# A 32-byte pad under the right side of SBUF in a rope attention and two-FFN kernel

## The chip, the core and the metric

The kernel runs on one core of one Trainium2 chip. The metric is the device time of one execution in microseconds, as a median over executions. The reference is computed in fp32; the kernel gets there by splitting fp32 operands into a high and a low part in the fp32r type and adding three products.

## What is computed

```python
# q, k, v: (4, 8, 576, 64)
q_rot, k_rot = rotate(q), rotate(k)                     # rope
attn = softmax(q_rot @ k_rot^T / 8)
x = (attn @ v) as (2304 tokens, 512)
h = x @ w_in      ; x = (h - tanh(h)) @ w_out           # w_in 512x2048, w_out 2048x512
h = x @ w_in2     ; out = (h * sigmoid(h)) @ w_out2
```

## The kernel before

**Attention** takes the 32 heads as 16 pairs. A pair has nine score tiles; each is built from 288-column matmuls of `qs` (stationary) with `kh` and `kl` (moving), lines 364, 365 and 371, and is followed by row maximum, exponential, transposes and the product with v. Even and odd pairs keep their rotated q and k in different pools: `qk_even` on the right side of SBUF, `qk_odd` on the left side. The rope work that builds them (pool `rope`) is on the right side too.

**The FFNs** are four passes p: passes 0 and 1 are the two halves of the first FFN's hidden dimension, passes 2 and 3 those of the second. A pass takes five token blocks kb in the order of the table `ORDER` (four of 512 tokens and block 4 with 256), and for each block eight slices f of 128 hidden units. One (p, kb, f) is a tick m, 160 in all. Tick m issues, on TensorE,

- `gemm_h(m)`, line 685: 12 matmuls hp <- x, w_in. Moving: `xh`, `xl` (512 columns, 256 in block 4). Stationary: `win`.
- `gemm_out(m - 4)`, line 761: in passes 0 and 1 12 matmuls with `gh`, `gl` moving and `wout` stationary; in passes 2 and 3 the roles are exchanged: `wout` moving, always 512 columns, and `gh`, `gl` stationary (12 matmuls, 6 in block 4).

Between them ScalarE and VectorE turn hp into g and its high and low parts (lines 696 to 730), and convert the next weights (lines 121 to 153). The order on each engine is written out by hand. An hp tile has four buffers, and `gemm_out` runs four ticks behind.

Where operands lie decides the case. The x of a block is split into `xh`, `xl` by `split` (lines 664 to 674), and line 666 alternates the pool from block to block:

```python
fp = pools["sb" if x % 2 == 0 else "x"]
```

`pools["sb"]` is `ffn`, on the right side; `pools["x"]` is `ffn_x`, on the left. The x of one block is kept where the next pass begins with the same block. So the pools go, in the order of the work:

| pass | blocks in order | pool of xh, xl |
|---|---|---|
| 0 | 0, 1, 4, 2, 3 | ffn, ffn_x, ffn, ffn_x, ffn |
| 1 | 3, 0, 1, 4, 2 | ffn, ffn_x, ffn, ffn_x, ffn |
| 2 | 0, 1, 4, 2, 3 | ffn_x, ffn, ffn_x, ffn, ffn_x |
| 3 | 3, 0, 1, 2, 4 | ffn_x, ffn, ffn_x, ffn, ffn_x |

`gh` and `gl` are always in `ffn`. The weights are in `wearly` and `wlate`, on the left. The first byte in a partition, as the pools give it out:

| tile (pool, side) | first byte before | modulo 64 |
|---|---|---|
| win, first slot (wearly, left) | 35520 | 0 |
| win, late slot (wlate, left) | 101056 | 0 |
| xh0 (ffn_x, left) | 158400 | 0 |
| xin (ffn, right) | 176096 | 32 |
| xh0 (ffn, right) | 184288 | 32 |
| gh (ffn, right) | 217056 | 32 |
| qs, kh (qk_odd, left) | 156544, 161152 | 0, 0 |
| qs, kh (qk_even, right) | 215008, 219616 | 32, 32 |

All tiles of a pool start at the same place modulo 64, and all steps inside them that a matmul takes (512 bytes in a weight or a g, 1152 and 2304 in q and k) are multiples of 64.

Of the kernel before, what the change touches and what calls it, by code (L numbers as in the profile page):

```python
# [8 lines left out]
F32 = mybir.dt.float32  # L9
# [20 lines left out]
def kernel(  # L30
# [43 lines left out]
    make_identity(nc, ident)  # L74
    sqa = const.tile([128, 1], F32, name="sqa")
    ht2 = const.tile([128, 1], F32, name="ht2")
    dram = ctx.enter_context(tc.tile_pool(name="dram", bufs=1, space=bass.MemoryType.DRAM))

    xd = [[dram.tile([128, KD, TW[kb]], F32, name=f"xd{l}{kb}") for kb in range(NBLK)] for l in range(2)]
# [820 lines left out]
```

## Time and profile before

| what | us |
|---|---|
| median of 3 runs (1147.18 to 1148.46) | 1147.21 |
| span of the profiled execution, first to last instruction | 1145.9 |
| TensorE busy in it | 1119.5 |
| VectorE busy | 785.3 |
| ScalarE busy | 659.2 |
| GpSimd busy | 268.4 |

The median of the timed runs is 1.3 us above the span of the profiled execution. TensorE's busy time is no measure of its use: matmuls overlap, a 512-column one is shown with some 394 ns while the next begins much sooner. The pace is read from the starts of successive matmuls in the timeline, which lists instructions in order of time and merges equal neighbours (x2). There a tick is the time from one first `hp<-xh` to the next.

### The profile page before, as it was taken

What the parts mean: (1) busy time and instruction counts of PE and PEld (TensorE: products, weight loads), DVE (VectorE), ACT (ScalarE), POOL (GpSimd) and SP (SyncE); (2) the same over time, 40 slices, a digit from 0 to 9 for tenths busy, and PEclk for the clock granted to TensorE, in tenths of its full rate; (3) what the DMA queues carried; (4) which work ended last, traced back from release to release, by engine and by line L of the source; (5) the groups of instructions that cost most, each with busy time, mean ns of one, the idle gap of its engine ahead of it and who ended that gap; (6) DMA issues with size and microseconds to landing.
All of it is one profiled execution on the core that took longest, in us unless ns stands there. A gap on an engine that the chain in (4) does not pass through costs nothing.

```text
span 1145.9 us, 16928 instructions
## 1 busy us (share of the span) xinstructions
PE 1119.5 (98%) x6032; PEld 902.6 (79%) x6032; DVE 785.3 (69%) x1385; ACT 659.2 (58%) x1431; POOL 268.4 (23%) x359
## 2 busy tenths in 40 slices
PE   5999999999999999999999999999999999999998
PEld 4777777777778889888888898888888888888887
DVE  7778788787858978888899979876544533323323
ACT  4888888788866757766666657534343323222221
POOL 6566676666300101111001001111000000000000
PEclk9999999999999999999999999999999999999999
DMA  4133323232311223221333332432232203122012
GB/s 130 47 99 84 113 68 110 89 94 86 100 64 42 92 74 111 96 89 56 111 129 110 111 120 84 147 111 92 75 110 74 74 1 111 37 74 93 31 44 74
DMA packets 69588, 98.94 MB, mean 86 GB/s; under 512 B 13952, under 2 KB 50432, under 8 KB 67712
## 3 DMA queue, kind: packets, MB, share of 16 engines
q1 hardware_dynamic: 69344, 97.61, 26.3%
q8 instruction: 47, 0.77, 0.3%
q14 instruction: 37, 0.30, 0.1%
q10 hardware_dynamic: 160, 0.26, 0.1%
HBM read 74.25 MB, written 23.59 MB: 85 GB/s over the span
## 4 chain that ended last, share of the span: by engine, by line
PE 91%; DVE 4%; ACT 3%; issue 1%; DMA 0%; SPq 0%; POOL 0%; DVEq 0%; ACTq 0%
PE acc L761 35%; PE hp L685 35%; PE x L498 7%; PE tpp L466 4%; PE sc L364 3%; PE sc L365 2%; PE tpq L332 2%; PE sc L371 1%; ACT p L391 1%; DVE st L377 1%; ACT kh L346 1%; PE sc L446 1%; PE tpb L418 0%; DMA xm<-in_q_dram 0%; DVE wa L136 0%
## 5 line engine op out<-in xcount | busy, mean ns | idle before, releaser
L685 PE MATMUL hp<-xh,win 128*128 128x512 f32 (+1 forms) x1280 | 391.7, 371 | 0.0
L696 ACT ACTIVATE t<-hp 128x512 f32<-128x512 f32 (+1 forms) x160 | 89.0, 557 | 409.7 <-PE hp L685 400.0
L730 DVE TENSOR_TENSOR gl<-t,gh 128x512 fp32r<-128x512 f32 (+1 forms) x160 | 105.9, 662 | 259.5 <-ACT gh L728 259.2
L685 PEld LDWEIGHTS hp<-xh,win 128*128 128x128 f32 x1280 | 233.7, 188 | 46.8 <-issue 1.3
L685 PE MATMUL hp<-xl,win 128*128 128x512 f32 (+1 forms) x640 | 237.0, 370 | 0.0
L761 PE MATMUL acc<-gh,wout 128*128 128x512 f32 (+1 forms) x640 | 196.7, 372 | 1.2 <-ACT u L700 1.2
L761 PE MATMUL acc<-wout,gh 128*128 128x512 f32 x576 | 181.0, 395 | 0.0
L377 DVE TENSOR_REDUCE st<-sc 128x1 f32<-128x576 f32 x144 | 108.7, 755 | 60.0 <-PE sc L446 34.9
L685 PEld LDWEIGHTS hp<-xl,win 128*128 128x128 f32 x640 | 120.2, 188 | 23.2
L761 PEld LDWEIGHTS acc<-gh,wout 128*128 128x128 f32 x640 | 116.7, 188 | 24.9 <-ACT u L700 1.6
L761 PEld LDWEIGHTS acc<-wout,gh 128*128 128x128 f32 x576 | 107.1, 188 | 24.4
L761 PE MATMUL acc<-gl,wout 128*128 128x512 f32 (+1 forms) x320 | 118.9, 372 | 0.0
L153 POOL TENSOR_TENSOR win<-wa,win 128x512 fp32r<-128x512 f32 x32 | 45.4, 1419 | 292.5 <-ACT win L149 292.5
L761 PE MATMUL acc<-wout,gl 128*128 128x512 f32 x288 | 113.8, 395 | 0.0
L391 ACT ACTIVATE p<-sc,st 128x576 f32<-128x576 f32 x144 | 107.0, 743 | 9.4 <-DVE pr L434 7.2
L153 POOL TENSOR_TENSOR wout<-wa,wout 128x512 fp32r<-128x512 f32 x32 | 43.8, 1367 | 284.2 <-ACT wout L149 272.5
L432 ACT ACTIVATE pt<-tpp 128x512 f32<-128x512 f32 x144 | 86.1, 598 | 28.2 <-PE tpp L466 27.4
L728 ACT ACTIVATE gh<-t 128x512 fp32r<-128x512 f32 (+1 forms) x160 | 93.7, 586 | 1.5 <-PE acc L761 1.5
L364 PE MATMUL sc<-kh,qs 128*128 128x288 f32 x256 | 85.4, 348 | 7.1 <-ACT p L391 5.1
L466 PE MATMUL tpp<-ident,p 128*128 128x128 f32 x576 | 87.1, 274 | 0.0
L498 PE MATMUL x<-pt,vm 128*64 128x256 f32 (+1 forms) x512 | 75.8, 418 | 2.1 <-DVE xs L507 1.9
L364 PEld LDWEIGHTS sc<-kh,qs 128*128 128x128 f32 x256 | 49.2, 192 | 34.2 <-ACT p L391 17.8
(112 smaller groups left out, 1798.5 us busy)
## 6 DMA issues: line engine op xcount, KB each, us to landing
raw<-in_moe_w_in_dram SPq DMA_DIRECT2D x32, 512.0 KB, 3.6
raw<-in_moe_w_out_dram SPq DMA_DIRECT2D x32, 512.0 KB, 3.6
xin<-xd SPq DMA_DIRECT2D x14, 1024.0 KB, 4.8
pd<-xo SPq DMA_DIRECT2D x34, 256.0 KB, 2.7
xo<-pd SPq DMA_DIRECT2D x34, 256.0 KB, 4.9
xm<-in_k_dram SPq DMA_DIRECT2D x16, 256.0 KB, 2.9
xm<-in_q_dram SPq DMA_DIRECT2D x16, 256.0 KB, 3.0
vm<-in_v_dram SPq DMA_DIRECT2D x16, 256.0 KB, 2.9
```

The source lines that it names most:

```text
L153: POOL.tensor_tensor(out=w[:, 1], in0=self.val.pop(j), in1=w[:, 0].bitcast(F32), op=ALU.subtract)
L364: PE.matmul(sc[:, e, 0:HALF], lhsT=l, rhs=kh[:, c], start=True, stop=False)
L377: DVE.tensor_reduce(out=st, in_=s_t[g][:, :, 0:HALF], op=ALU.max, axis=AX.XY, negate=True)
L391: ACT.activation(out=p.rearrange("p (e s) -> p e s", e=2), in_=sc[:, :, 0:HALF], func=ACTF.Exp, bias=st, accum_out=sum_t[i][:, n:n + 1])
L432: ACT.activation(out=dst, in_=src, func=ACTF.Copy)
L466: PE.transpose(tp[:, cc * 128:(cc + 1) * 128], p[:, p0 + cc * 128:p0 + (cc + 1) * 128], ident)
L498: PE.matmul(x[o, 0:w], lhsT=l, rhs=r, start=(cc == 0), stop=(cc == NJ))
L685: PE.matmul(hp, lhsT=w[:, a, ws], rhs=bb, start=(n == 0), stop=(n == 3 * KD - 1))
L696: ACT.activation(out=t, in_=hp, func=ACTF.Tanh, scale=0.5 if l else 1.0)
L728: ACT.activation(out=gh, in_=t, func=ACTF.Copy)
L730: DVE.tensor_tensor(out=gl, in0=t, in1=gh.bitcast(F32), op=ALU.subtract)
L761: PE.matmul(acc, lhsT=a, rhs=bb, start=(fi == 0 and n == 0), stop=(fi == NH - 1 and n == 2))
```

## The change

A pool with one tile of 8 fp32 elements (32 bytes in each partition) is opened on the right side of SBUF before all other pools of that side. The right side grows downwards, so every tile on it (pools `qk_even`, `rope`, `ffn`) starts 32 bytes lower: xh0 at 184256, gh at 217024, kh of the even pairs at 219584, all multiples of 64. The left side does not move. No instruction reads or writes the pad; every engine has the same instructions in the same order with the same waits as before.

```diff
@@ -74,6 +74,8 @@
     make_identity(nc, ident)
     sqa = const.tile([128, 1], F32, name="sqa")
     ht2 = const.tile([128, 1], F32, name="ht2")
+    right_pad = ctx.enter_context(tc.tile_pool(name="right_pad", bufs=1, side="right"))
+    right_pad.tile([128, 8], F32, name="pad_right")
     dram = ctx.enter_context(tc.tile_pool(name="dram", bufs=1, space=bass.MemoryType.DRAM))
```

## Rows read from the trace of the kernel before

**Rows 1.** The page: span, lines of the chain that ended last, granted TensorE clock.

```profile
span 1145.9 us, 16928 instructions
...
PE acc L761 35%; PE hp L685 35%; PE x L498 7%; PE tpp L466 4%; PE sc L364 3%; PE sc L365 2%; PE tpq L332 2%; PE sc L371 1%; ACT p L391 1%; DVE st L377 1%; ACT kh L346 1%; PE sc L446 1%; PE tpb L418 0%; DMA xm<-in_q_dram 0%; DVE wa L136 0%
```

**Rows 2.** TensorE's waits from 345 us on: releaser, total us, times, longest.

```profile
PE acc L761 <- ACT u L700: 1.2, 1, 1.2
```

**Rows 3.** Timeline of TensorE in pass 3, block 0 (x in ffn): start, us, instruction.

```profile
979.09 0.39 PE L685 MATMUL hp<-xh,win 128*128 128x512 f32 x1
979.32 0.40 PE L685 MATMUL hp<-xl,win 128*128 128x512 f32 x1
...
981.66 0.39 PE L685 MATMUL hp<-xh,win 128*128 128x512 f32 x1
981.89 0.63 PE L761 MATMUL acc<-wout,gh 128*128 128x512 f32 x2
...
984.69 0.39 PE L685 MATMUL hp<-xh,win 128*128 128x512 f32 x1
```

**Rows 4.** Timeline of TensorE in pass 2, block 3 (x in ffn_x).

```profile
896.12 0.39 PE L685 MATMUL hp<-xh,win 128*128 128x512 f32 x1
896.35 0.39 PE L685 MATMUL hp<-xl,win 128*128 128x512 f32 x1
...
898.62 0.40 PE L685 MATMUL hp<-xh,win 128*128 128x512 f32 x1
...
901.65 0.39 PE L685 MATMUL hp<-xh,win 128*128 128x512 f32 x1
```

**Rows 5.** Timeline of TensorE in pass 1, block 2 (x in ffn): one gemm_out.

```profile
714.58 0.40 PE L761 MATMUL acc<-gh,wout 128*128 128x512 f32 x1
...
717.38 0.40 PE L685 MATMUL hp<-xh,win 128*128 128x512 f32 x1
```

**Rows 6.** Timeline of TensorE in pass 0, block 1 (x in ffn_x): one tick.

```profile
374.76 0.40 PE L685 MATMUL hp<-xh,win 128*128 128x512 f32 x1
...
380.32 0.40 PE L685 MATMUL hp<-xh,win 128*128 128x512 f32 x1
```

**Rows 7.** Timeline of TensorE, 256 columns: pass 0 block 4 (ffn), pass 3 block 4 (ffn_x).

```profile
430.51 0.28 PE L685 MATMUL hp<-xh,win 128*128 128x256 f32 x1
...
433.34 0.28 PE L685 MATMUL hp<-xh,win 128*128 128x256 f32 x1
...
1108.26 0.40 PE L685 MATMUL hp<-xh,win 128*128 128x256 f32 x2
...
1108.74 0.63 PE L761 MATMUL acc<-wout,gh 128*128 128x512 f32 x2
```

**Rows 8.** Timeline of TensorE in attention: first scores of pairs 8 to 12.

```profile
169.38 0.40 PE L364 MATMUL sc<-kh,qs 128*128 128x288 f32 x1
...
189.04 0.40 PE L364 MATMUL sc<-kh,qs 128*128 128x288 f32 x1
...
208.99 0.38 PE L364 MATMUL sc<-kh,qs 128*128 128x288 f32 x1
...
229.14 0.38 PE L364 MATMUL sc<-kh,qs 128*128 128x288 f32 x1
...
248.56 0.38 PE L364 MATMUL sc<-kh,qs 128*128 128x288 f32 x1
```

**Rows 9.** Waits of the other engines from 345 us on.

```profile
ACT t L696 <- PE hp L685: 394.6, 150, 4.5
...
DVE gl L730 <- ACT gh L728: 256.5, 111, 4.3
```

**Rows 10.** Busy us by engine from 540 to 640 us: PE, PEld, DVE, ACT, POOL, then clock.

```profile
540.00:640.00 100.00, 100.00 (x432) 80.61 (x431) 91.06 (x143) 66.97 (x122) 12.33 (x9) 1.00 0.33 107
```

## Prediction

> **What bounds the kernel now.** I read the chain first, then TensorE's waits, then the spacing of its matmuls. In the chain that ended last two FFN lines alone hold 70% of the span, 761 and 685, both on TensorE [rows 1]. From 345 us to the end TensorE waits once, for 1.2 us [rows 2]; the other engines wait for it instead: ScalarE 394.6 us in 150 waits for hp, VectorE 256.5 us in 111 waits for ScalarE's gh [rows 9]. So the FFN, the last 800 of the 1145.9 us, lasts as long as TensorE takes to issue its matmuls, and a nanosecond off each of them comes off the end. [...]
>
> The pace is the thing to look at, and the kernel holds its own experiment: the same instructions with x on the right side in some blocks and on the left in others. **x in ffn (32 modulo 64).** From the second to the twelfth matmul of a gemm_h, ten steps, 979.32 to 981.66: 234 ns each. The gemm_out behind it, weights moving from the left and g stationary from the right, 981.89 to 984.69: 2.80 us over twelve, 233.3 ns. The whole tick is 984.69 - 979.09 = 5.60 us, 24 times 233.3 ns [rows 3]. **x in ffn_x (0 modulo 64).** Ten steps from 896.35 to 898.62: 227 ns. The tick is 901.65 - 896.12 = 5.53 us [rows 4]; its gemm_out, still with a g at 32 modulo 64, takes the same 2.80 us, so its gemm_h takes 2.73. **g moving (32 modulo 64), weights stationary.** 714.58 to 717.38, 2.80 us over twelve, again 233.3 ns [rows 5].
>
> So a 512-column matmul takes 233.3 ns when either operand, moving or stationary, starts at 32 modulo 64, and about 227 when both start at 0. [...] Other engines are no explanation: the fast rows 4 and the slow rows 3 are both from the second FFN with the same work beside them, and in passes 0 and 1, where VectorE is busy 91.06 of 100 us [rows 10], the slow pace is the same 233.3 [rows 5].
>
> **The change part by part.** No instruction, wait or order changes; addresses on the right side drop by 32 bytes, and all FFN operands come to 0 modulo 64, the state of the fast rows. There are 128 ticks with 512-token blocks and 32 with 256.
>
> *Slow 512-column matmuls.* gemm_h with x in ffn: 72 ticks of 12, 864. gemm_out of passes 0 and 1: 64 of 12, 768. gemm_out of passes 2 and 3: 64 of 12 and 16 of 6, 864. Together 2496, each from 233.3 to 226.7: 2496 x 6.6 ns = 16.5 us, all on TensorE's path.
>
> *Fast 512-column matmuls.* 56 ticks already have x in ffn_x, but they begin behind a slow gemm_out and settle only after some matmuls. In passes 0 and 1 such a tick is 5.56 us [rows 6], so its gemm_h is 5.56 - 2.80 = 2.76 us against 12 x 226.7 ns = 2.72; in passes 2 and 3 it is 2.73 [rows 4]. With 24 ticks of the first kind, five at the start of pass 2 that go like them, and 27 of the second: 29 x 0.04 + 27 x 0.01 = 1.4 us, since no slow neighbour is left.
>
> *256-column matmuls.* Here the phase works the other way. With x and g in ffn a tick in block 4 is 433.34 - 430.51 = 2.83 us for 24, 118 ns each; the settled pace with x in ffn_x is (1108.74 - 1108.26) / 4 = 120 ns [rows 7]. There are 32 ticks of 12 in gemm_h and 16 of 12 in gemm_out of passes 0 and 1, 576 in all; at about 1.8 ns each they lose 1.0 us. Bounds: 0 and 1.2 us (576 x 2 ns).
>
> *Attention.* The even pairs' q and k and the rope tiles move; the odd pairs show what they move to. Pair 8 takes 19.66 us, 9 19.95, 10 20.15, 11 19.42: even 19.91, odd 19.69 [rows 8]. Eight even pairs at 0.22 less would be 1.8 us. But the scatter between two pairs of one kind (0.49 and 0.53) is over twice that, so it may as well be nothing, or a loss: the bounds are a gain of 1.8 and, of the same size because the scatter has no sign, a loss of 1.8. I take 0, the middle of the two.
>
> *The other engines.* VectorE, ScalarE and GpSimd get the same work in less time. In the densest stretch VectorE is busy 91.06% [rows 10]; at a pace 2.9% quicker (5.44 in place of 5.60 us a tick) that is 93.8%, so it still fits. The one wait of 1.2 us [rows 2] stands where pass 1 goes from block 4 to block 2 and the accumulators must be read by VectorE first; TensorE comes there sooner, VectorE a little less so. I estimate 0.2 us more wait, with bounds of 0 and of the 1.3 us that the eight ticks of the block before the small one save (8 x 0.16).
>
> Sum: 16.5 + 1.4 - 1.0 + 0 - 0.2 = 16.7 us off the span of 1145.9, which gives 1129.2. The median stands 1.3 us above the span, and nothing in the change touches what lies outside: 1147.2 - 16.7 = **1130.5 us**.
>
> **The rivals.** *It is the place, not the phase (no change).* In the fast rows both operands are also on the left side, and their distance is a multiple of 512 bytes; afterwards all of ffn is still on the right, 256 bytes off in that measure. If place or such a distance sets the pace, the 2496 stay at 233.3 ns: at most 1.0 us (256 columns) is lost, 1147.2 to 1148.2. For it: the FFN rows never separate side from phase. Against it: passes 1 and 3 mix the early and late weights with both sorts of x and keep the paces, and inside a gemm_h the weights' slices lie 0, 512, 1024 and 1536 bytes on without any step in the settled pace. [...] Chance 0.10.
>
> *Only part of the pairs speeds up.* If a g that is stationary is slow for its own reason (it is written shortly before it is loaded) and not for its phase, the 864 of passes 2 and 3 stay slow: 864 x 6.6 ns = 5.7 us less, 1136.2. The same follows if VectorE, at 93.8%, begins to hold TensorE in passes 0 and 1. For it: 91% is an average, single ticks are fuller. Against: hp's four buffers and four ticks of lag, and 256.5 us that VectorE waits. Chance 0.09.
>
> *Slower: both streams in step.* [...] Chance 0.03.
>
> **How the numbers follow.** Forecast as worked out: 0.78. Its own ends are the unknowns of attention (1.8 either way), the stall (up to 1.1 more) and the fast pace (544 cycles or the 227.0 of the rows, 1.0 us): about 1128 to 1134. The range should leave out two in ten at most; it takes in the partial rival, with the same unknowns, and leaves the others: 1127.5 to 1138. A measurement of this kernel can tell about 0.2%, 2.3 us, from no change: forecast and partial rival lie beyond it, 0.87 faster; no change 0.10; slower 0.03.
>
> **What would show it.** In the changed kernel's timeline a 512-column tick of any block should be 5.44 us, ten settled steps 2.27, and a tick of block 4 in passes 0 and 1 2.88. If ticks with x in ffn stay at 5.60, place was the cause; if gemm_h goes to 2.72 and gemm_out of passes 2 and 3 stays at 2.80, the stationary side is the partial rival's. If ticks are 5.44 but waits appear on TensorE in passes 0 and 1, VectorE has become the bound. Attention's pairs should not differ by more than their scatter. A slow tick above 5.60 would make me wrong in sign.

## The result, and the profile after

| kernel | median of runs, us | span of the profiled execution, us |
|---|---|---|
| before | 1147.20 (1146.99 to 1148.46) | 1145.9 |
| after | 1131.81 (1130.64 to 1132.00) | 1129.9 |

The ratio is 0.9861, with a 95% interval of 0.9847 to 0.9875: 1.4% faster, 15.4 us in the median and 16.0 in the span. The forecast was 1130.5. The cause that the forecast gave, each operand's own place modulo 64, is not the right one, though; the experiments below show that, for 512-column matmuls whose operands begin on multiples of 32 bytes, what counts is the distance between the two operands, and modulo 256: 226.7 ns a matmul at a distance of 0, 228.9 to 234.3 at the seven other multiples of 32.

The page of the changed kernel, its span and the lines of the chain, answering to [rows 1] (line numbers are 2 higher than before):

```profile
span 1129.9 us, 16928 instructions
...
PE 1102.6 (98%) x6032; PEld 902.8 (80%) x6032; DVE 784.2 (69%) x1385; ACT 658.4 (58%) x1431; POOL 268.9 (24%) x359
...
PE acc L763 34%; PE hp L687 34%; PE x L500 7%; PE tpp L468 4%; PE sc L366 4%; PE sc L367 2%; PE tpq L334 2%; PE sc L373 1%; ACT p L393 1%; DVE st L379 1%; ACT kh L348 1%; PE sc L448 1%; PE tpb L420 0%; DMA xm<-in_q_dram 0%; DVE wa L138 0%
```

Only TensorE's busy time has changed, by 16.9 us; the other engines have the same to about 1 us, and the two FFN lines still hold 68% of the span in the chain.

The timeline of TensorE in the changed kernel (start, us, instruction) shows the first matmul of each gemm_h (687) and gemm_out (763): a tick of pass 3, block 0, with x in ffn, against [rows 3]; one of pass 2, block 3, with x in ffn_x, against [rows 4]; one of pass 1, block 1, with g moving, against [rows 5]; one of pass 0, block 4, against [rows 7]:

```profile
971.99 0.39 PE L687 MATMUL hp<-xh,win 128*128 128x512 f32 x1
...
974.71 0.39 PE L763 MATMUL acc<-wout,gh 128*128 128x512 f32 x1
...
977.43 0.39 PE L687 MATMUL hp<-xh,win 128*128 128x512 f32 x1
...
884.95 0.39 PE L687 MATMUL hp<-xh,win 128*128 128x512 f32 x1
...
890.39 0.39 PE L687 MATMUL hp<-xh,win 128*128 128x512 f32 x1
...
619.97 0.39 PE L687 MATMUL hp<-xh,win 128*128 128x512 f32 x1
...
622.69 0.39 PE L763 MATMUL acc<-gh,wout 128*128 128x512 f32 x1
...
625.41 0.39 PE L687 MATMUL hp<-xh,win 128*128 128x512 f32 x1
...
431.38 0.28 PE L687 MATMUL hp<-xh,win 128*128 128x256 f32 x1
...
434.26 0.28 PE L687 MATMUL hp<-xh,win 128*128 128x256 f32 x1
```

Every 512-column tick shown is now 5.44 us (977.43 - 971.99, 890.39 - 884.95, 625.41 - 619.97), both halves 2.72, whichever operand moves: 226.7 ns a matmul. The tick of block 4 has become slower, 2.88 us where it was 2.83.

The waits from 345 us on (releaser, total us, times, longest), first TensorE's, then the other engines', against [rows 2, 9], and 100 us of the first FFN as busy us by engine, against [rows 10]:

```profile
PE acc L763 <- DVE xo L773: 1.3, 1, 1.3
```

```profile
ACT t L698 <- PE hp L687: 377.8, 151, 4.3
...
DVE gl L732 <- ACT gh L730: 243.2, 107, 4.2
```

```profile
529.00:629.00 100.00, 100.00 (x443) 82.81 (x442) 92.59 (x146) 68.73 (x125) 14.10 (x10) 1.00 0.35 114
```

The others wait 13 to 17 us less for TensorE and its results, and VectorE is at 92.59 of 100 us where it was at 91.06. That is not its densest stretch; a denser one in each kernel, first before, then after, is

```profile
560.00:660.00 100.00, 100.00 (x433) 80.70 (x432) 93.03 (x145) 64.79 (x118) 13.26 (x10) 1.00 0.35 117
...
556.00:656.00 100.00, 100.00 (x448) 83.02 (x448) 94.80 (x149) 66.21 (x123) 13.62 (x10) 1.00 0.38 125
```

93.03 and 94.80 us. Even so VectorE does not hold TensorE anywhere but in the one wait, 1.3 us where it was 1.2. The starts of pairs 8 to 12 in attention, against [rows 8]:

```profile
169.17 0.40 PE L366 MATMUL sc<-kh,qs 128*128 128x288 f32 x1
...
188.86 0.40 PE L366 MATMUL sc<-kh,qs 128*128 128x288 f32 x1
...
208.85 0.38 PE L366 MATMUL sc<-kh,qs 128*128 128x288 f32 x1
...
228.97 0.38 PE L366 MATMUL sc<-kh,qs 128*128 128x288 f32 x1
...
248.40 0.38 PE L366 MATMUL sc<-kh,qs 128*128 128x288 f32 x1
```

19.69, 19.99, 20.12 and 19.43 us, where they were 19.66, 19.95, 20.15 and 19.42: attention gained nothing, though the even pairs' operands moved. All but 0.3 us of the span's gain lies in the FFN: from the first start of a gemm_h to the end of the last matmul it took 813.4 us and takes 797.7.

### The profile page after: what moved, and what is told of

It is laid out like the page before. It is cut to its first block, busy times and chain, and to the rows that moved or that the text cites. A ratio compares the mean times of both kernels' runs of the same rounds, so it can differ in the third digit from the quotient of the medians.

```text
span 1129.9 us, 16928 instructions
## 1 busy us (share of the span) xinstructions
PE 1102.6 (98%) x6032; PEld 902.8 (80%) x6032; DVE 784.2 (69%) x1385; ACT 658.4 (58%) x1431; POOL 268.9 (24%) x359
## 4 chain that ended last, share of the span: by engine, by line
PE 90%; DVE 5%; ACT 3%; issue 1%; DMA 0%; SPq 0%; POOL 0%; DVEq 0%; ACTq 0%
PE acc L763 34%; PE hp L687 34%; PE x L500 7%; PE tpp L468 4%; PE sc L366 4%; PE sc L367 2%; PE tpq L334 2%; PE sc L373 1%; ACT p L393 1%; DVE st L379 1%; ACT kh L348 1%; PE sc L448 1%; PE tpb L420 0%; DMA xm<-in_q_dram 0%; DVE wa L138 0%
## 5 line engine op out<-in xcount | busy, mean ns | idle before, releaser
L687 PE MATMUL hp<-xh,win 128*128 128x512 f32 (+1 forms) x1280 | 387.6, 368 | 0.0
L763 PE MATMUL acc<-gh,wout 128*128 128x512 f32 (+1 forms) x640 | 193.8, 368 | 1.3 <-DVE xo L773 1.3
L763 PE MATMUL acc<-wout,gh 128*128 128x512 f32 x576 | 177.8, 390 | 0.0
L763 PE MATMUL acc<-gl,wout 128*128 128x512 f32 (+1 forms) x320 | 117.8, 368 | 0.0
```

What stands on the lines that cost most here:

```text
L687: PE.matmul(hp, lhsT=w[:, a, ws], rhs=bb, start=(n == 0), stop=(n == 3 * KD - 1))
L763: PE.matmul(acc, lhsT=a, rhs=bb, start=(fi == 0 and n == 0), stop=(fi == NH - 1 and n == 2))
```

## The experiments

The phase of an operand is its first byte modulo 64; a pair in brackets gives the stationary operand's bytes first, then the moving one's. The forecast's theory was A: a matmul is slow if either operand begins off a multiple of 64. The rivals: B, it is slow if the two phases differ; C, it is the side of SBUF or some larger distance. Later ones are named where they came up.

### Matmuls alone: phases of the two operands

The kernel is a loop of matmuls on two tiles; x and w are filled once, nothing else runs beside them.

```python
def series(nm, ws, xs, cols, reps):
    nonlocal n
    w, x, size = ops[nm]
    for r in range(reps):
        w0, x0 = ws // size + r % 4 * 128, xs // size
        PE.matmul(hp[n % 4][:, 0:cols], lhsT=w[:, w0:w0 + 128],
                  rhs=x[:, r % 2, x0:x0 + cols], start=True, stop=True)
        n += 1
```

> A kernel of matmuls alone: 512 moving columns, fp32r, each with its own 128x128 stationary operand, no other engine at work; 36 series of 32, the stationary operand 0, 16, 32 or 48 bytes and the moving one 0, 4, 8, 16, 24, 32, 40, 48 or 56 bytes past a multiple of 64. It leaves out the whole computation. [...] Theory B (unequal phases collide): 226.7 ns where the two phases are equal, (16, 16), (32, 32), (48, 48) too, 233.3 elsewhere. Theory C (side of SBUF or distance of the operands): no difference between the series, since all lie in the same two tiles.

Measured, as the mean from start to start over the last 23 steps of each series, in ns (rows: the stationary operand's bytes; columns: the moving one's):

| | 0 | 4 | 8 | 16 | 24 | 32 | 40 | 48 | 56 |
|---|---|---|---|---|---|---|---|---|---|
| 0 | **226.7** | 236.7 | 233.5 | 231.6 | 233.3 | 233.3 | 233.1 | 233.3 | 229.9 |
| 16 | 233.3 | 236.7 | 233.5 | 233.3 | 233.4 | **226.7** | 233.5 | 232.3 | 232.2 |
| 32 | 233.3 | 236.3 | 233.3 | 236.8 | 230.0 | **226.7** | 233.5 | 231.6 | 233.3 |
| 48 | 233.3 | 240.0 | 231.2 | **226.7** | 236.6 | **226.7** | 233.7 | 233.3 | 233.3 |

With no other engine at work both paces of the kernel stand there, so neither needs the work of another engine. Theory C, as a matter of the side, is out: all series use the same two tiles. Theory A, by which (0, 0) alone would be fast, is out too: (32, 32) takes the same 226.7 ns. Theory B holds for phases 0 and 32, the only ones in the kernel, but not for the others: (16, 16) and (48, 48) are slow, 233.3 ns, (16, 32) fast, 226.7.

### Matmuls alone: width and type

The same loop with the widths and with a bf16 pair of tiles added to the list of series.

> As the kernel of matmuls alone, with phases (0, 0), (0, 32), (32, 0), (32, 32) of stationary and moving operand, for 512, 448, 384, 320, 288, 256 and 128 columns, in fp32r and then in bf16. It leaves out the whole computation. [...]

| columns, fp32r | (0, 0) | (0, 32) | (32, 0) | (32, 32) |
|---|---|---|---|---|
| 512 | 226.7 | 233.3 | 233.3 | 226.7 |
| 448 | 202.8 | 206.7 | 204.4 | 206.7 |
| 384 | 173.3 | 173.3 | 173.4 | 173.4 |
| 320 | 146.7 | 146.7 | 146.6 | 146.7 |
| 288 | 131.6 | 133.4 | 133.4 | 131.6 |
| 256 | 120.0 | 117.9 | 118.4 | 120.0 |
| 128 | 111.7 | 111.6 | 111.7 | 111.7 |

The cost of unequal phases, 6.6 ns at 512 columns, is no fixed charge: nothing at 384 and 320 columns, 1.7 ns at 288, and at 256 equal phases lose 1.6 to 2.1 ns, as block 4 does in the kernel (2.88 us a tick after, 2.83 before). At 448 columns (0, 0) and (32, 32) differ by 3.9 ns, so there neither equal phases nor any rule by distance alone fits, and the pattern is that of theory A. Attention did not move, and this fits: qs and kh of an even pair lie in one pool, 4608 bytes apart before and after, so the pad moves both from 32 to 0, and at 288 columns (32, 32) and (0, 0) are alike, 131.6 ns. In bf16 a 512-column matmul took 215.8 ns at all four pairs of phases, and no width from 448 to 128 showed a difference of 0.1 ns: at these places the effect belongs to fp32r.

### x alone brought to a multiple of 64

```diff
     def on_scores_near():
         for c in range(KD):
             split(0, c)
+        pools["sb"].tile([128, 8], F32, name="pad_ffn")
```

> The pad lies inside pool ffn, behind xin, xh and xl: these begin at multiples of 64, while t, u, s, mk, gh, gl and all of attention's right side stay at 32 past one. Theory A (each operand's own phase counts): gemm_out stays at 2.80 us in all passes, gemm_h with x in ffn goes from 2.80 to 2.73 to 2.76, the figures of x in ffn_x before; 72 of them, 2.9 to 5.0 us less: 1142 to 1144.5 us. Theory C (side of SBUF): nothing changes, 1147.2 us.

1144.00 us, ratio 0.9970 (0.9959 to 0.9981). A tick of pass 3, block 0, from the timeline (gemm_h, gemm_out, next gemm_h):

```profile
982.25 0.39 PE L685 MATMUL hp<-xh,win 128*128 128x512 f32 x1
...
984.98 0.39 PE L761 MATMUL acc<-wout,gh 128*128 128x512 f32 x1
...
987.78 0.39 PE L685 MATMUL hp<-xh,win 128*128 128x512 f32 x1
```

gemm_h 2.73 us with x in ffn, gemm_out still 2.80: the figures of [rows 4]. So moving the one operand speeds up its own matmuls alone, on the right side of SBUF as on the left; theories A and B both say so, and C, as a matter of the side, is out for the kernel too. A larger distance is not out: x in ffn_x and x here are both a multiple of 256 bytes from the weights.

### All operands at 32 past a multiple of 64

```diff
+    left_pad = ctx.enter_context(tc.tile_pool(name="left_pad", bufs=1))
+    left_pad.tile([128, 8], F32, name="pad_left")
     stage = ctx.enter_context(tc.tile_pool(name="stage", bufs=1))
```

> Instead of the right side, the left side moves by 32 bytes: all operands, weights, x, g, q, k, begin at 32 past a multiple of 64. Theory A (own phase): the 56 ticks with x in ffn_x lose what they had, every 512-column tick is 5.60 us: 56 x 0.04 to 0.07 = 2.2 to 4 us more, 1149.4 to 1151 us. Theory B (unequal phases collide): every tick is 5.44 us as after the change, 1131 us.

1131.18 us, ratio 0.9859 (0.9843 to 0.9876), with none of the FFN's operands on a multiple of 64. The same tick:

```profile
972.34 0.39 PE L687 MATMUL hp<-xh,win 128*128 128x512 f32 x1
...
975.06 0.39 PE L763 MATMUL acc<-wout,gh 128*128 128x512 f32 x1
...
977.78 0.39 PE L687 MATMUL hp<-xh,win 128*128 128x512 f32 x1
```

2.72 and 2.72. This is the change's whole gain without its alignment, and theory A falls with it: it had 1149.4 to 1151 here. What the two kernels share is the distance between the operands.

### Other pads on the right side

Only the size of the pad differs from the changed kernel. The 24 elements shown are 96 bytes; the other runs have 16, 72, 40 and 56 elements for 64, 288, 160 and 224 bytes.

```diff
-    right_pad.tile([128, 8], F32, name="pad_right")
+    right_pad.tile([128, 24], F32, name="pad_right")
```

> Right pad of 96 bytes: the right side at a multiple of 64 again, but 64 bytes lower than after the change, so that its distance to the weights is off by 64 modulo 128 and modulo 256. Theory B' (what counts is the distance of the two operands modulo 64): ticks of 5.44 us, 1130.5 to 1132 us as after. Theory D (a multiple of 128 or 256 is needed): ticks with an operand in ffn at 5.60, about 1147 us.

> Right pad of 64 bytes: the pad is there and everything on the right moves, but its phase stays 32 past a multiple of 64. Theory B': as before the change, 5.60 us ticks with x in ffn, 1146.5 to 1148 us. Theory E (the moved place or the room at the end of SBUF helps): about 1131 us.

64 bytes: 1147.19 us, ratio 0.9997 (0.9987 to 1.0006). A pad as such does nothing. 96 bytes: 1142.81 us, ratio 0.9959 (0.9944 to 0.9974), and this was expected by no theory: every operand on a multiple of 64, as after the change, and a third of the gain (theory D had the slow ticks, but no gain). Its timeline in pass 1, block 1, and then a tick of pass 2, block 3, with x in ffn_x:

```profile
623.89 0.39 PE L687 MATMUL hp<-xh,win 128*128 128x512 f32 x1
...
626.70 0.39 PE L763 MATMUL acc<-gh,wout 128*128 128x512 f32 x1
...
629.50 0.39 PE L687 MATMUL hp<-xh,win 128*128 128x512 f32 x1
...
893.00 0.39 PE L687 MATMUL hp<-xh,win 128*128 128x512 f32 x1
...
895.72 0.62 PE L763 MATMUL acc<-wout,gh 128*128 128x512 f32 x2
...
898.47 0.39 PE L687 MATMUL hp<-xh,win 128*128 128x512 f32 x1
```

2.81 and 2.80 us with x and g moving, the slow pace, but 2.75 us with w moving: gemm_out of passes 2 and 3 gave 2.5 us in all, most of the gain. So multiples of 64 are not enough. The matmuls alone were asked for larger distances:

> Matmuls alone again, 512 columns in fp32r; the whole computation is left out. First distances of a multiple of 64 (stationary 0, moving 64 to 256; 64 and 128 against 0; 32 against 96): 226.7 ns at all of them if only the distance modulo 64 counts, 0 against 96 at 233.3. Then ten of the first scan's pairs in reverse order: the same paces as there (226.7 at (48, 32), (48, 16), (32, 32), (16, 32), (0, 0)) if they belong to the addresses, others if they hang on what ran before. [...] Then 496, 480 and 464 columns: where between 512 and 448 the difference of the phases sets in.

| stationary, moving | 0, 64 | 0, 96 | 0, 128 | 0, 192 | 0, 256 | 64, 0 | 128, 0 | 32, 96 | 96, 32 |
|---|---|---|---|---|---|---|---|---|---|
| ns | 229.0 | 233.4 | 232.4 | 233.4 | **226.7** | 233.4 | 232.8 | 229.0 | 233.4 |

0 and 256 are fast, 64, 128 and 192 are not. This made theory F: the distance from the stationary to the moving operand modulo 256 sets the pace. (In the loop the slices of w lie 512 bytes apart and the two rows of x 2304, which is 9 x 256, so a series has one distance modulo 256.) F holds for places that are multiples of 32 alone: in the first scan (16, 16), at distance 0, was slow, and (48, 16), at 224, fast. In these terms the kernel before had 184288 - 35520 = 148768 = 581 x 256 + 32 between x in ffn and w, the change took the 32 away, and 96 bytes leave 192 (moving x or g) and 64 (moving w, stationary g).

The rest of this run is mixed. In reverse order (48, 16), (16, 32), (32, 32) and (0, 0) were at 226.7 (the last at 226.8) again, but (48, 32) was at 233.3 where it had been at 226.7, and (16, 16) and (48, 48) at 231.1 where they had been at 233.3: for steps of 16 bytes the places alone do not fix the pace. What ran before is one difference between the two runs, the chip another. With stationary operands of 128, 96, 64 and 32 columns at (0, 0) and (0, 32) it was 226.7 and 233.3 ns, 230.0 and 233.3, 230.0 and 230.8, 231.7 and 232.5: the difference shrinks from 6.6 to 0.8 ns with the stationary operand's columns, while the faster of the two paces rises from 226.7 to 231.7. Whether the weight load takes part in this was not shown. With 496, 480 and 464 columns (0, 0) and (0, 32) lie 1 ns apart, and (32, 0) 3 ns above (0, 0).

Theory F was then put to the kernel with three more pads, and to the matmuls alone with all distances in steps of 32.

> Right pad of 288 bytes, 256 more than the change. Theory F (the distance of moving and stationary operand modulo 256 sets the pace; the change brought it from 32 to 0): distance 0 again, ticks of 5.44 us, 1131 to 1132.3 us. Theory G (it fits only at the change's own addresses, modulo 512 or more): ticks of 5.60, up to 1147 us.

> Right pad of 160 bytes, 128 more than the change: all operands still begin on a multiple of 64. Theory F: distance 128 both ways round, for which the matmuls alone gave 232.4 and 232.8 ns: ticks with x in ffn about 5.58 us, 2496 x 0.8 ns = 2 us off before, 1144 to 1146.5 us. Theory B' (distance modulo 64) or the same modulo 128: 5.44 us ticks, 1131 to 1132 us.

> Right pad of 224 bytes, 192 more than the change, again all on multiples of 64. Theory F: moving x or g lies 64 past the stationary weight (modulo 256), 229.0 ns in the matmuls alone, and in passes 2 and 3 the moving weight 64 before the stationary g, 233.4 ns: gemm_h with x in ffn and gemm_out of passes 0 and 1 at 2.75 us, gemm_out of passes 2 and 3 at 2.80; 1632 x 4.3 ns = 7 us off before: 1139 to 1141.5 us. The mirror image of the 96-byte pad. Theory B': 1131 to 1132 us.

> Matmuls alone in fp32r, the whole computation left out: 512, 256, 288 and 320 columns, the moving operand 0, 32, ... 224 bytes past the stationary one modulo 256. At 512 columns theory F expects the figures seen so far: 226.7 at 0, 233.3 at 32, 229.0 at 64, 233.4 at 96, 232.4 at 128, 233.4 at 192 and, from the exchanged roles, 233.3 at 224; 160 is open. At 256 columns 120 ns at 0 and 117.9 at 32, and from the kernel with the 96-byte pad, whose gemm_h of block 4 with x in ffn took 1.365 us for 12, about 113.8 at 192. Open: whether any distance beats 0 at 512 columns, or 113.8 at 256.

The timeline of the last, 22 steps each (9th to 31st matmul of a series) at distances 0, 64 and 192:

```profile
26.38 0.62 PE L60 MATMUL hp<-xr,wr 128*128 128x512 f32 x2
...
31.36 0.61 PE L60 MATMUL hp<-xr,wr 128*128 128x512 f32 x2
...
41.12 0.62 PE L60 MATMUL hp<-xr,wr 128*128 128x512 f32 x2
...
46.16 0.62 PE L60 MATMUL hp<-xr,wr 128*128 128x512 f32 x2
...
70.92 0.63 PE L60 MATMUL hp<-xr,wr 128*128 128x512 f32 x2
...
76.06 0.63 PE L60 MATMUL hp<-xr,wr 128*128 128x512 f32 x2
```

(31.36 - 26.38) / 22 = 226, (46.16 - 41.12) / 22 = 229 and (76.06 - 70.92) / 22 = 234 ns, to the rows' rounding. All eight, with 512 and 256 columns:

| moving minus stationary, modulo 256 | 0 | 32 | 64 | 96 | 128 | 160 | 192 | 224 |
|---|---|---|---|---|---|---|---|---|
| 512 columns, ns | **226.7** | 233.3 | 228.9 | 233.4 | 233.5 | 234.3 | 233.2 | 233.3 |
| 256 columns, ns | 120.0 | 117.9 | 117.8 | 120.1 | 118.9 | 117.3 | **113.4** | 118.3 |

At 288 columns the eight lie between 131.6 and 133.4, at 320 they are all 146.6 to 146.8. No distance beats 0 at 512 columns. The kernel by pad, beside the pace that the matmuls alone give for its two distances:

| right pad, bytes | moving x or g from w, modulo 256 | ns alone | moving w from g | ns alone | kernel, us | ratio to before |
|---|---|---|---|---|---|---|
| 0 (before) | 32 | 233.3 | 224 | 233.3 | 1147.2 | 1 |
| 32 (after) | 0 | 226.7 | 0 | 226.7 | 1131.81 | 0.9861 (0.9847 to 0.9875) |
| 64 | 224 | 233.3 | 32 | 233.3 | 1147.19 | 0.9997 (0.9987 to 1.0006) |
| 96 | 192 | 233.2 | 64 | 228.9 | 1142.81 | 0.9959 (0.9944 to 0.9974) |
| 160 | 128 | 233.5 | 128 | 233.5 | 1147.07 | 0.9997 (0.9988 to 1.0007) |
| 224 | 64 | 228.9 | 192 | 233.2 | 1142.71 | 0.9957 (0.9941 to 0.9974) |
| 288 | 0 | 226.7 | 0 | 226.7 | 1131.69 | 0.9860 (0.9846 to 0.9875) |

The timeline of the kernel with 224 bytes, in pass 1, block 1, and then a gemm_out of pass 3:

```profile
621.74 0.39 PE L687 MATMUL hp<-xh,win 128*128 128x512 f32 x1
...
624.48 0.39 PE L763 MATMUL acc<-gh,wout 128*128 128x512 f32 x1
...
627.23 0.39 PE L687 MATMUL hp<-xh,win 128*128 128x512 f32 x1
...
981.82 0.39 PE L763 MATMUL acc<-wout,gh 128*128 128x512 f32 x1
...
984.62 0.40 PE L687 MATMUL hp<-xh,win 128*128 128x512 f32 x1
```

2.74 and 2.75 us with x and g moving, 2.80 with w moving, the mirror image of 96 bytes, as theory F has it. At 288 bytes the time is the change's again, so theory G is out. The sizes were less well met: 160 bytes came out at no gain where 1 to 3 us were expected (128 apart was 232.4 in one run of the matmuls alone and 233.5 in the next), and 224 bytes at 1142.7 where 1139 to 1141.5 were expected. There a gemm_h with x in ffn takes 2.76 and 2.80 us in turn where its neighbour is a slow gemm_out (pass 3, block 0), and the 56 with x in ffn_x lost 0.7 us in all. So the distance sets the pace of a long run of like matmuls, and the neighbours still shift it where gemms of two paces alternate.

### Block 4 at the distance that suits 256 columns

```diff
+        if w < T:
+            hi, lo = hi[:, 48:48 + w], lo[:, 48:48 + w]
...
-        gh, gl = tmp(m, "gh", 3, F32R), tmp(m, "gl", 3, F32R)
+        o, w = 48 * (SEQ[m][0] < 2 and TW[SEQ[m][1]] < T), TW[SEQ[m][1]]
+        gh, gl = (pools["sb"].tile([128, T], F32R, tag=n, name=n, bufs=3)[:, o:o + w] for n in ("gh", "gl"))
```

> The changed kernel, and in block 4 xh and xl, and in passes 0 and 1 gh and gl, lie 192 bytes further in their tiles, so that the 256-column moving operands are 192 bytes past their weights modulo 256, where the matmuls alone took 113.4 ns in place of 120. Theory F: gemm_h of block 4 and gemm_out of it in passes 0 and 1 go from 1.43 to about 1.36 us, 48 of them, 3.4 us; at the borders to the 512-column matmuls beside them up to 0.02 us each is given back: 1128.3 to 1130 us. If the pace of 256 columns in the kernel is set by its neighbours and not by the distance: 1131 to 1132 us.

1130.33 us (1129.03 to 1130.72), ratio 0.9848 (0.9835 to 0.9862), between the two expected ranges. Its interval overlaps that of the change, so the timed runs do not tell the two apart; the span is 1127.8 against 1129.9, of which the 256-column matmuls gave 1.0 us and the 512-column ones 0.8. A tick of pass 0, block 4:

```profile
430.88 0.28 PE L689 MATMUL hp<-xh,win 128*128 128x256 f32 x1
...
433.71 0.28 PE L689 MATMUL hp<-xh,win 128*128 128x256 f32 x1
```

2.83 us, 118 ns a matmul, not the 113.4 of the matmuls alone. In the kernel with the 96-byte pad, whose x has the very same distance of 192, this tick was

```profile
431.93 0.28 PE L687 MATMUL hp<-xh,win 128*128 128x256 f32 x1
...
434.65 0.28 PE L687 MATMUL hp<-xh,win 128*128 128x256 f32 x1
```

2.72 us, 113.3 ns. So at 256 columns the same distance has two settled paces in two kernels, and theory F does not cover this width. Known differences are the 512-column matmuls ahead of the block, slow in one kernel and fast in the other; the distance modulo 512, 192 there and 448 here (the matmuls alone alternate between these two and keep 113.4 ns); and the chip. What picks the pace stays open.

## Why the prediction was right, and where it was not

- **What bounds the kernel.** Right. TensorE alone held the end of the FFN, and what came off its matmuls came off the span. The stretch that the forecast called VectorE's densest was not (93.03 against 91.06), but VectorE still fits, with 94.80 of 100 us after.
- **The sum.** The 512-column matmuls that were slow gave 15.4 us (from 579.8 to 564.4 over the 2486 steps that no wait and no attention interrupts), forecast 16.5; those that were fast 1.2, forecast 1.4; the 256-column ones lost 0.8, forecast 1.0; the wait grew by 0.1, forecast 0.2; attention 0, as forecast. The rows behind the forecast show 227 ns for the fast pace, not the 226.7 that the sum takes, and no run shows the 544 cycles that the range has for it; the matmuls alone later ran at 226.7. The first term is the mis-sized one: the mean was 233.2 and became 227.0, not 226.7, because 28 of the gemm_h and gemm_out concerned follow a 256-column one and still take 0.03 us longer, as in pass 0, block 4:

```profile
417.40 0.40 PE L763 MATMUL acc<-gh,wout 128*128 128x512 f32 x1
...
420.15 0.28 PE L687 MATMUL hp<-xh,win 128*128 128x256 f32 x1
```

  2.75 us for twelve. The 0 for attention was the middle of two bounds and came true by luck: the reason, that both operands of a score matmul move together, was not in the forecast, which let the odd pairs show what the even ones move to. The median fell by 15.4 us and the span by 16.0. The forecast's 1.3 us between the two compared a median with the span of another execution; in the runs on record each execution lies 1.7 to 2.9 us above its own span, and the difference of 0.6 us is within that scatter.
- **The cause: the failed step.** It is the sentence that "a 512-column matmul takes 233.3 ns when either operand, moving or stationary, starts at 32 modulo 64, and about 227 when both start at 0". The rows on the pace were read rightly, but they held only two states, and in the fast one the operands were at 0 modulo 64 and also at a distance of 0 modulo 256. With all operands at 32 the kernel is as fast (1131.18 us); with all at 0 but 64, 128 or 192 bytes apart it is not (1142.7 to 1147.1). The number came true with the wrong cause, by luck, because 32 bytes happened to close the distance: for x in ffn from 148768 to 148736, which is 581 times 256.
- **The rivals.** *Place, not phase* was given 0.10 and held half of the truth. The side of SBUF plays no part (gemm_h takes 2.73 us with x on the right in the run with x alone moved, and 2.73 on the left [rows 4]); a larger distance does, though 256 and not the 512 that was named (288 bytes of pad, 256 more than the change, gave 1131.69 us). The argument against it, that weights' slices 512 bytes on show no step, only excluded distances beyond 512. *Only part of the pairs* did not happen with this pad, but it is what 96 and 224 bytes do (1142.81 and 1142.71 us). *Both streams in step*, the slower kernel at 0.03, did not happen either: at 512 columns equal phases of 0 or 32 give the quicker pace, 226.7 against 233.3 ns. At 256 columns they do not: 120.0 ns at distance 0, 113.4 to 118.9 at six of the seven others, and the 256-column matmuls lost 0.8 us.
- **What would show it.** All of the ticks named for the forecast (5.44 us, 2.27 for ten steps, 2.88 in block 4) were met, and none of them could tell theory A from theory F. A prediction with a list of signs that only its own rivals fail is not yet a test of the cause.

## What to carry to other kernels

Where fp32r matmuls with 512 moving columns follow each other without a gap, read the pace from their starts, and compare blocks whose operands lie differently: 226.7 and 233.3 ns a matmul were 1.4% of this kernel, and a pad of 32 bytes decided between them. Try the moving operand at a multiple of 256 bytes from the stationary one, both on multiples of 32: here that took 226.7 ns, and the other multiples of 64 were not enough (228.9 ns at 64, 233.5 at 128, 233.2 at 192). This is for 512 columns: at 256 that distance was among the slowest (120.0 ns, the others 113.4 to 120.1). When a trace offers a natural experiment, ask what else differs between its two states, and break them apart (here: shift both operands) before giving the cause a name.

## What the runs showed of the hardware

- The pace of back-to-back fp32r matmuls depends on where the moving and the stationary operand lie to each other: at 512 columns, with both on multiples of 32, 226.7 ns at distance 0 modulo 256, 228.9 at 64, 232.4 to 234.3 at the other multiples of 32. At 448 columns distance 0 gave 202.8 at one place and 206.7 at another, and at 256 columns another distance was the fastest (113.4 ns at 192, 120.0 at 0). With no other engine at work, moving either operand by 32 bytes costs 6.6 ns (226.7 to 233.3), and moving both costs nothing (226.7). What in the chip couples them was not found; with fewer stationary columns the difference shrinks (6.6 ns at 128, 0.8 at 32), and the pace does not fall (226.7 ns at 128, 231.7 at 32, both at distance 0).
- In bf16 the same loop took 215.8 ns a matmul at 512 columns, at each of the four pairs of phases. A weight load took 191 ns in fp32r and 98 in bf16; the two by line, count, busy us and mean ns:

```profile
L60 PEld LDWEIGHTS hp<-xr,wr 128*128 128x128 f32 x960 | 149.5, 191 | 17.8 <-ACT xr L50 7.1
L60 PEld LDWEIGHTS <-wb 128*128 128x128 bf16 x896 | 82.3, 98 | 44.6
```

- A pace, once settled, repeats (5.44 or 5.60 us a tick over whole blocks of 512 columns, after or before the change), but for some places two were seen: 113.3 or 117.8 ns for 256 columns at distance 192, 226.7 or 233.3 at phases 48 and 32. What ran before differed in each case, and so did the chip; the two were not told apart. The kernel before ran alike on all four chips (medians of 1147.21 to 1147.74 us).
